# Rows stored once in float32 and split where a block gathers them, and early blocks' three products summed in one PSUM region

## The chip, the cores and the metric

The kernel runs on one core of one Trainium2 chip. That core has a matrix engine (TensorE, called PE in the profile), three engines for elementwise work (VectorE is DVE, ScalarE is ACT, GpSimd is POOL) and SyncE (SP), whose queue issues most of the transfers. The metric is the device time of one execution in microseconds; lower is better. Matrix products accumulate in PSUM, everything else lies in SBUF or, through DMA, in DRAM.

## The reference

Three layers follow one another. Attention with 8 batches, 8 heads, 576 tokens and head size 64 goes through 32 packed queries per head: `p_packed = sm_attn(p, k, v)` and `out = sm_attn(q, p_packed, p_packed)`. A dense layer takes the 4608 tokens of width 512: `h = max(x @ w1, x @ w2, x @ w3)`, then `y = h @ w_out`. The last layer picks one of 8 experts per token:

```python
logits = x @ w_gate
e_idx = np.argmax(logits, axis=1)
...
gate_w = probs[np.arange(N), e_idx]
eom = 1.0 / (1.0 + np.exp(-(x @ w_output_gate)))
for e in range(E):
    mask = e_idx == e
    ...
    h = np.maximum(x[mask] @ w1[e], 0.0)
    ye = h @ w2[e]
    out[mask] = gate_w[mask, None] * eom[mask, e, None] * ye
```

Inputs and output are float32. The kernel keeps that accuracy with float16 products by splitting a number into a high half (its float16 rounding) and a low half (what is left), and by adding three products: high with high, high with low, low with high. `PASS` in the code is that list.

## The kernel before

The first stage goes through the eight batches. For each batch the program forms scores, the packed result (`att_pv`: 4 groups of heads, each a chain of 15 matrix products over 5 chunks of keys, of which the fifth, `vt16`, has 64 keys where the others have 128), the second softmax, and the dense layer: `att_g` makes products G of the packed values with the three weights, `mm1` multiplies them by the attention weights and takes the maximum, and `mm2` multiplies a tile of 128 tokens by `w_out`, with the two gates' weights folded in as 16 more columns. There are 36 such tiles; each takes 36 products of 264 columns and a two-bank PSUM buffer `pss`, of which there are two, shared with the third product of `mm1` and with the scores.

What `mm2` does with a finished tile is the row store. Before the change, a tile was made ready for float16 work at once: the largest magnitude is found (`peak`, on ACT or DVE), a factor is worked out (`bound`, two small DVE steps), ACT writes the scaled high half (`row(0)`), ACT writes the 16 logits, DVE writes the scaled low half (`less` into `row(1)`) and only then gives the PSUM buffer back, POOL writes the factor and copies 8 logits to `LG`. The row of 512 high halves, 512 low halves, 16 logits and a factor goes to the DRAM table `yrow`. For the last five tiles (`busy`) the halves are made through an SBUF copy `ys` and POOL makes the low half.

The second stage is the expert layer in blocks of 128 tokens of one expert. From `LG` the program works out each token's expert and place (`chosen`, `ranked`, `rows_hot`, `inverse`: a matrix product of one-hot rows, line 377 of the profile, gives each block's list of tokens). This happens first for the first 27 tiles, which fills blocks 0 to 3, and then for all 36, which gives the lists of blocks 4 to 36. A block gathers its rows from `yrow` by an indirect DMA (`fetch`, POOL), transposes them by DMA (`turn_rows`), multiplies by the expert's first weights (`hidden`, two halves `fq`), takes the positive part and splits it, and multiplies by the second weights (`outer`). Its result is scaled by `gates` and sent to the output (`send`). Block i's `outer` stands on PE behind block i+1's `hidden`. The expert weights are split beforehand into the DRAM table `wscr` in 8 parts for each expert (`part_load`, `part_hi`, `part_lo`, `part_store`); for the rarer experts this is done beside the early blocks (`beside`).

In `hidden` before the change a 128-row weight block multiplies both halves of the rows at once (256 columns), then the low weights multiply the high halves (128 columns). High-with-low lands in a PSUM region of its own, so the two regions are added afterwards: `second` copies one to SBUF on ACT, `both` adds the other on DVE, then `relu_hi` (ACT) and `relu_lo` (DVE) run from SBUF.

The order of the first stage and of blocks 0 to 3 on every engine is set when the program is built: the class `Flow` takes steps with costs and ranks and lays them out one after another. The table `T_` holds its numbers. Where it sees PE pausing it inserts products of ones whose result nobody uses (`fill`, line 253). Each engine then runs its list in order. From block 4 on the order is written out by hand.

## Time and profile before

| what | value |
|---|---|
| median of 3 runs | 1019.18 us (1016.92 to 1020.22) |
| the profiled execution | 1020.05 us, of which 1018.3 us from the first to the last instruction |
| PE busy | 927.3 us, 91% of the span |
| DVE, ACT, POOL busy | 652.5, 468.6, 407.6 us |
| mean granted PE clock | 0.964 of 2.4 GHz |

A matrix product's busy time in the profile is modelled and overlaps its neighbours', so the distance between starts tells more than the duration of one. An engine that works is not always the one that sets the end: what counts is which engine is waited for in a given stretch. The profile's chain of what ended last only follows the final 50 us of transfers, so the rows below come from other views.

### The profile page before, as it was taken

The page shows a single profiled execution, that of the slowest core. Times are in us where ns is not written, and L with a number is a line of the kernel's source. Part 1 is how long each engine was busy: PE and PEld are TensorE (multiplying, and loading weights), DVE is VectorE, ACT ScalarE, POOL GpSimd, SP SyncE. Part 2 cuts the span into 40 slices and gives each one's busy share as a digit, 9 for nine tenths or more (in the row PEclk, how much of TensorE's full clock was granted, in tenths as well). Part 3 has the DMA queues.
Part 4 walks back from the last instruction along what each step waited for, and adds up shares of the span by engine and source line. Part 5 has one row for each costly group of instructions (what it writes and reads, how often), then busy time and mean ns, then how long its engine had stood idle before and what let it go on. Part 6 is the DMA issues. An engine that isn't in the chain of part 4 may idle for free. (4 is left out here: it accounts for less than half of the span.)

```text
span 1018.3 us, 23704 instructions
## 1 busy us (share of the span) xinstructions
PE 927.3 (91%) x8697; PEld 673.8 (66%) x8697; DVE 652.5 (64%) x1590; ACT 468.6 (46%) x1018; POOL 407.6 (40%) x542
## 2 busy tenths in 40 slices
PE   8879987899898797988999997999999999999995
PEld 6556764677676575766768785667676766767672
DVE  3999886745757378889695539577785344443431
ACT  4545745545555445454434353455563333333331
POOL 0534854724766368666743262223222211212110
PEclk9989998999999897989899998999999999999998
DMA  9896397570767759978912376832223593324930
GB/s 282 275 266 176 79 199 162 130 197 11 174 129 162 160 162 254 266 252 236 254 43 69 141 200 252 264 98 75 75 74 96 166 309 74 85 73 118 286 109 25
DMA packets 220985, 164.41 MB, mean 161 GB/s; under 512 B 156031, under 2 KB 195967, under 8 KB 217792
## 3 DMA queue, kind: packets, MB, share of 16 engines
q1 hardware_dynamic: 214944, 143.38, 53.2%
q0 software_dynamic: 5920, 19.46, 5.7%
q8 instruction: 70, 1.15, 0.5%
q14 instruction: 51, 0.42, 0.1%
HBM read 240.35 MB, written 53.00 MB: 288 GB/s over the span
## 5 line engine op out<-in xcount | busy, mean ns | idle before, releaser
L1024 PEld LDWEIGHTS <-G 128*128 128x128 f16 x1728 | 170.8, 100 | 84.2 <-issue 34.9
L1365 PE MATMUL pso<-wbuf,h 128*128 128x512 f16 x816 | 181.7, 379 | 0.0
L1024 PE MATMUL psm<-A,G 128*128 128x288 f16 x1152 | 167.1, 295 | 11.0 <-ACT t L197 5.1
L1062 PE MATMUL pss<-wo,hT 128*128 128x264 f16 x1296 | 152.8, 280 | 7.8 <-DVE row L217 4.3
L1314 PE MATMUL psh<-xT,wbuf 128*128 128x256 f16 x1056 | 158.5, 273 | 0.5 <-DMA wbuf<-wscr 0.5
L1365 PEld LDWEIGHTS <-h 128*128 128x128 f16 x888 | 85.3, 98 | 96.5 <-issue 0.3
L1062 PEld LDWEIGHTS <-hT 128*128 128x128 f16 x1296 | 128.4, 99 | 31.1 <-issue 10.4
L1375 POOL DMA_INDIRECT out<-o,sidx x33 | 39.5, 1198 | 259.0 <-ACT o L1370 254.6
L215 POOL TENSOR_TENSOR hT<-t,hT 128x288 f16<-128x288 f32 x89 | 72.0, 810 | 121.3 <-ACT hT L197 98.7
L1314 PEld LDWEIGHTS <-wbuf 128*128 128x128 f16 x1184 | 105.0, 98 | 17.3 <-DMA wbuf<-wscr 2.4
L1328 DVE TENSOR_TENSOR hs<-psh,hs 128x512 f32<-128x512 f32 x66 | 45.5, 690 | 90.3 <-ACT hs L197 86.5
L1024 PE MATMUL pss<-A,G 128*128 128x288 f16 x576 | 88.7, 292 | 15.0 <-ACT e L805 6.1
L1316 PE MATMUL psh<-xT,wbuf 128*128 128x128 f16 x1056 | 102.0, 219 | 0.0
L1316 PEld LDWEIGHTS <-wbuf 128*128 128x128 f16 x1184 | 91.5, 98 | 6.8
L1336 DVE SCALAR_TENSOR_TENSOR h<-hs,h 128x512 f16<-128x512 f32 x74 | 51.2, 692 | 48.8 <-ACT h L1333 48.7
L1333 ACT ACTIVATE h<-hs 128x512 f16<-128x512 f32 x74 | 46.5, 629 | 59.8 <-DVE hs L1328 59.0
L1033 DVE SCALAR_TENSOR_TENSOR t<-psm,t 128x288 f32<-128x288 f32 x96 | 43.4, 453 | 45.2 <-PE psm L1024 31.2
L197 ACT ACTIVATE hs<-psh 128x512 f32<-128x512 f32 x66 | 39.2, 594 | 63.9 <-PE psh L1316 63.9
L197 ACT ACTIVATE hT<-t 128x288 f16<-128x288 f32 x81 | 35.7, 440 | 69.2 <-DVE t L1033 69.1
L197 ACT ACTIVATE G<-psm 128x384 f16<-128x384 f32 x96 | 43.6, 485 | 32.8 <-PE psm L996 25.3
L217 DVE SCALAR_TENSOR_TENSOR G<-psm,G 128x384 f16<-128x384 f32 x96 | 49.8, 545 | 8.4 <-ACT G L197 7.8
L197 ACT ACTIVATE t<-psm 128x288 f32<-128x288 f32 x96 | 38.6, 402 | 33.3 <-PE psm L1024 24.6
(294 smaller groups left out, 1466.2 us busy)
## 6 DMA issues: line engine op xcount, KB each, us to landing
wbuf<-wscr SPq DMA_DIRECT2D x148, 1024.0 KB
pt<-in_moe_w SPq DMA_DIRECT2D x40, 512.0 KB
wscr<-po SPq DMA_DIRECT2D x40, 512.0 KB
pl<-in_moe_w SPq DMA_DIRECT2D x48, 256.0 KB
wscr<-po SPq DMA_DIRECT2D x48, 256.0 KB
ld<-in_k SPq DMA_DIRECT2D x14, 512.0 KB
ld<-in_q SPq DMA_DIRECT2D x14, 512.0 KB
ld<-in_v SPq DMA_DIRECT2D x12, 512.0 KB
```

The lines of the kernel that those rows point to most:

```text
L197: act.activation(out=o, in_=i, func=AF.Copy, scale=scale)
L215: engines[e].tensor_tensor(out=o, in0=i, in1=hi, op=ALU.subtract)
L217: dve.scalar_tensor_tensor(out=o, in0=i, scalar=scale, in1=hi, op0=ALU.mult, op1=ALU.subtract)
L1024: pe.matmul(ps()[:, 0:288], lhsT=a.G[ft]()[:, g, lg, w * 128:(w + 1) * 128], rhs=a.A16()[:, g, la, c * 288:(c + 1) * 288], start=(n == 0), ...
L1033: e0 = add(costs(288, dve=1), lambda e, src=src, o=o: dve.scalar_tensor_tensor(out=o()[:], in0=src(), scalar=sc, in1=t0()[:], op0=ALU.mult ...
L1062: pe.matmul(view()[:, nh, 0:OG0], lhsT=hT()[:, ft, lh, c0:c0 + 128], rhs=wo16()[:, ft, lw, nh, :], start=(i == 0 and ft == 0), stop=(i == ...
L1314: pe.matmul(o.rearrange("r (l t) -> r l t", l=2), lhsT=w1v[:, kt, 0, cols], rhs=xT[:, :, kt, :], start=(kt == 0), stop=False)
L1316: pe.matmul(o[:, 0:128], lhsT=w1v[:, kt, 1, cols], rhs=xT[:, 0, kt, :], start=False, stop=(kt == 3))
L1328: dve.tensor_tensor(out=hv, in0=parts_of(ps)[:, :, 0, :], in1=hv, op=ALU.add)
L1333: act.activation(out=h2_part(h2, fq, 0), in_=ps[:], func=AF.Relu)
L1336: dve.scalar_tensor_tensor(out=h2_part(h2, fq, 1), in0=ps[:], scalar=0.0, in1=h2_part(h2, fq, 0), op0=ALU.max, op1=ALU.subtract)
L1365: pe.matmul(po, lhsT=h2[:, lh, ft, :], rhs=w2v[:, ft, lw, :], start=(n == 0), stop=(n == 23))
```

## The change

Six edits go together.

- `mm2` stores a row in float32 in one step (`put`, ACT or DVE): two halves of 264, each 256 values and 8 logits, scaled by `FC`. POOL or ACT copies 8 logits to `LG`. Nothing is split there, and the five last tiles go the same way.
- A block scales and splits its rows after the gather: `bound` (a DVE reduction and two small steps), `row_hi` (ACT), `row_lo` (DVE), then the transposing DMA. `gates` takes the factor from `bound`.
- Blocks 0 to 13 sum the three products in one PSUM region (`hidden`: 12 products of 128 columns for each 128 outputs), and `relu_hi` and `relu_lo` read PSUM. Blocks from 14 on keep the old form, now `hidden_apart` and `summed`.
- The fifth chunk of `att_pv` has its lower 64 rows filled with zeros (a POOL memset for each of 6 batches), and all 15 products use 128 rows.
- Four of the eight parts of the fourth expert's weights move from the planned stage to block 4, and the fifth expert's parts from blocks 4 to 6 to blocks 5 and 6.
- A few numbers of `T_` change, so the planner lays the first stage out anew.

```diff
-T_ = dict(fg=0.597, ff=0.42, fm=2.856, rk=2.0, ...
+T_ = dict(fg=0.597, ff=0.42, fm=2.856, rk=0.088, ...
...
-            out = []
+            out = [add(dict(pool=0.4), lambda e: pool.memset(a.v16()[1][64:128], 0.0), after=[opened], rank=rank)]
...
-                        kk = 128 if t < 4 else 64
-                        vs = a.v16()[0][:, lv, t, 2 * hp:2 * hp + 2, :] if t < 4 else a.v16()[1][:kk, lv, 2 * hp:2 * hp + 2, :]
+                        vs = a.v16()[0][:, lv, t, 2 * hp:2 * hp + 2, :] if t < 4 else a.v16()[1][:, lv, 2 * hp:2 * hp + 2, :]
                         pe.matmul(ps()[:, hp * 64:hp * 64 + 64], lhsT=vs,
-                                  rhs=a.PT()[:kk, hp // 2, lp, t, (hp % 2) * 64:(hp % 2) * 64 + 64],
+                                  rhs=a.PT()[:, hp // 2, lp, t, (hp % 2) * 64:(hp % 2) * 64 + 64],
...
-            def bound(e):
-                dve.tensor_scalar(out=am()[:], in0=am()[:], scalar1=1e-30, scalar2=2.0 ** -8 if by[0] == "act" else 0.25,
-                                  op0=ALU.max, op1=ALU.mult)
-                dve.reciprocal(out=rs()[:], in_=am()[:])
...
+            def put(e):
+                o = rf().rearrange("r (n c) -> r n c", n=2)
                 if e == "act":
...
+                    act.activation(out=o, in_=view()[:, :, 0:OG0], func=AF.Copy, scale=FC[:, t:t + 1])
                 else:
...
+                    dve.tensor_scalar(out=o, in0=view()[:, :, 0:OG0], scalar1=FC[:, t:t + 1], scalar2=None, op0=ALU.mult)
+            y = add(costs(ROW, act=1, dve=1), put, after=[prev], rank=rank + V('y', batch), take=(rf,), give=(ps,))
+            f = add(dict(pool=0.25, act=0.2), lambda e: scaled(e, LG[:, t, :], rf()[:, 256:OG0]), after=[y], rank=rank + V('y', batch))
...
+    def bound(i):
+
+        am[i], rs = sm_.tile([128, 1], F32, tag="am", name="bam", bufs=6), sm_.tile([128, 1], F32, tag="rs", name="brs")
+        dve.tensor_reduce(out=am[i][:], in_=y_of(G_[i]), op=ALU.max, axis=AX.XY, apply_absolute_value=True)
+        dve.tensor_scalar(out=am[i][:], in0=am[i][:], scalar1=1e-30, scalar2=0.25, op0=ALU.max, op1=ALU.mult)
+        dve.reciprocal(out=rs[:], in_=am[i][:])
+        return rs
+
+    def row_hi(i, x, rs):
+        act.activation(out=half(x, 0), in_=y_of(G_[i]), func=AF.Copy, scale=rs[:])
+
+    def row_lo(i, x, rs):
+        less("dve", half(x, 1), y_of(G_[i]), half(x, 0), rs[:])
...
     def hidden(i, xT, fq, ps):
+
+        w1v = wbuf[i % 2][:, 0:8192].rearrange("r (a l f) -> r a l f", a=4, l=2)
+        for f4 in range(4):
+            cols = slice((fq * 4 + f4) * 128, (fq * 4 + f4 + 1) * 128)
+            for n, (lw, lx) in enumerate(PASS):
+                for kt in range(4):
+                    pe.matmul(ps[:, f4 * 128:(f4 + 1) * 128], lhsT=w1v[:, kt, lw, cols], rhs=xT[:, lx, kt, :],
+                              start=(n + kt == 0), stop=(n == 2 and kt == 3))
...
+        y = add(dict(dve=0.95), lambda e: rs.append(bound(i)), after=[y], rank=1)
+        y = add(dict(act=0.65), lambda e: row_hi(i, x(), rs[0]), after=[y], rank=1, take=(x,))
+        y = add(dict(dve=0.7), lambda e: row_lo(i, x(), rs[0]), after=[y], rank=1)
+        turned[i] = add(dict(sp=0.6), tr, after=[y], rank=1, move=0.9, give=(x,))
...
-    for u in range(8):
-        part_steps(NP1, u, found + [opened])
+
+    for i in range(NE):
+        hidden_steps(i)
+        if i == 1:
+            for u in range(4):
+                part_steps(NP1, u, hid[i] + [opened])
...
+                if i in beside:
+                    hidden(i, X_[i], fq, ps)
+                else:
+                    hidden_apart(i, X_[i], fq, ps)
+                    ps = summed(ps)
...
         for i in range(NE, NBLK0):
+            if i + 1 in split:
+                X_[i + 1] = turn_rows(split[i + 1])
+            parts_out()
             cur = block(i)
-            parts_out()
+            if i + 3 < NBLK0:
+                G_[i + 3] = fetch(i + 3)
+            if NE + 2 < i + 2 < NBLK0:
+                split[i + 2] = split_rows(i + 2)
             parts_made(i)
-            if i + 3 < NBLK0:
-                gather(i + 3)
```

PE's list where the blocks begin, first before the change: line 1365 is block 0's `outer`, line 253 the fill, line 377 the product that gives the lists of blocks 4 and up, line 1314 block 2's `hidden`.

```order
L1365 MATMUL psm<-wbuf_8766,h_9214 128x512
L253 LDWEIGHTS ones_62
L253 MATMUL psv<-ones_62 128x128
...
L377 LDWEIGHTS er_8771
L377 MATMUL psv<-fu_8781,er_8771 128x78
...
L1314 LDWEIGHTS wbuf_8766
L1314 MATMUL pss<-xT,wbuf_8766 128x256
```

And now, at the same place: line 1309 is block 2's `hidden`.

```order
L1309 LDWEIGHTS wbuf_8543
L1309 MATMUL pss<-xT,wbuf_8543 128x128
L377 LDWEIGHTS er_8548
L377 MATMUL psv<-fu_8558,er_8548 128x78
...
L1309 LDWEIGHTS wbuf_8543
L1309 MATMUL pss<-xT,wbuf_8543 128x128
```

The 40 fill products between block 0's `outer` and line 377 are gone, the first half of block 2's `hidden` (48 products) stands there instead, and the second half follows line 377.

POOL's list at the same place, before: line 373 forms one of the two operands (`fu`) of line 377, line 1375 is `send`, line 1298 `fetch`.

```order
L1095 COPY LG<-row 128x8
L215 TENSOR_TENSOR row<-ys,row 128x512
L332 MEMSET goes_8772 128x80
L333 MEMSET goes_8772 128x8
L1375 DMA out<-o,gidx_66 4608x512
L373 TENSOR_TENSOR fu_8781<-fq_8780,tokb 128x36x39
L1298 DMA g<-yrow,gidx 128x529 x2
```

And now (`send` is line 1377, `fetch` line 1267):

```order
L204 TENSOR_SCALAR LG<-row 128x8 x3
L332 MEMSET goes_8549 128x80
L333 MEMSET goes_8549 128x8
L373 TENSOR_TENSOR fu_8558<-fq_8557,bat_104 128x36x39
L1377 DMA out<-o,gidx_66 4608x512
L1267 DMA g<-yrow,gidx 128x528 x2
```

The operand is now made ahead of block 0's `send`, no low half of a row is made on POOL, and it is the other operand that POOL makes; DVE makes this one.

DVE's list where the second count begins, before: line 316 ends the choice of experts for the last nine tiles, lines 342 and 343 are the running count, lines 1328 and 1336 are `both` and `relu_lo`.

```order
L316 CAST oh_8770<-over 128x72
L1328 TENSOR_TENSOR hs<-pss,hs 128x512
L1336 SCALAR_TENSOR_TENSOR h_9214<-hs,h_9214 128x512
L1328 TENSOR_TENSOR hs<-pss,hs 128x512
L342 COPY inc_8773<-cnt 128x8
L343 SCALAR_TENSOR_TENSOR run_8774<-goes_8772,inc_8773 128x80
```

And now: line 1337 is `relu_lo`, lines 1346 to 1359 are block 0's `gates`.

```order
L316 CAST oh_8547<-over 128x72
L1337 SCALAR_TENSOR_TENSOR h_8982<-pss,h_8982 128x512 x2
L342 COPY inc_8550<-cnt 128x8
L1346 TENSOR_REDUCE bmx<-g 128x1
...
L1359 SCALAR_TENSOR_TENSOR bfac<-bfac,bam 128x1
L343 SCALAR_TENSOR_TENSOR run_8551<-goes_8549,inc_8550 128x80
```

Both `relu_lo` of block 0 and its whole `gates` now stand ahead of the running count, while no `both` is left there.

## Rows read from the trace of the kernel before

**Rows 1.** The page's first part: busy time of PE.

```profile
PE 927.3 (91%) x8697; PEld 673.8 (66%) x8697; DVE 652.5 (64%) x1590; ACT 468.6 (46%) x1018; POOL 407.6 (40%) x542
```

**Rows 2.** Windows: length, busy PE, PEld, DVE, ACT, POOL, clock, DMA.

```profile
0.00:604.34 604.34, 533.67 (x5363) 399.71 (x5364) 427.95 (x915) 299.44 (x676) 321.28 (x466) 0.95 0.68 177
604.34:654.35 50.01, 42.79 (x408) 32.09 (x406) 37.25 (x100) 20.32 (x39) 13.19 (x11) 0.93 0.78 275
654.35:1008.00 353.65, 350.86 (x2929) 242.01 (x2927) 187.31 (x575) 148.88 (x304) 73.08 (x66) 1.00 0.44 124
```

**Rows 3.** Window: an early stretch of the first stage, same columns.

```profile
24.00:96.00 72.00, 60.34 (x620) 41.28 (x621) 70.20 (x139) 37.49 (x87) 31.65 (x37) 0.93 0.87 248
```

**Rows 4.** Timeline of PE in a run of `att_pv`: start, length, products.

```profile
429.83 0.29 PE L864 MATMUL psv<-PT,v 128*128 128x64 f16 x4
430.05 0.20 PE L864 MATMUL psv<-PT,vt 64*128 64x64 f16 x1
430.18 0.29 PE L864 MATMUL psv<-PT,v 128*128 128x64 f16 x4
```

**Rows 5.** Line 864: its products on 64 rows; durations in ns.

```profile
L864 PE MATMUL psv<-PT,vt x72: 199/200/233, 136.9 to 490.7; 64*128 64x64 f16 x72
```

**Rows 6.** Timeline of DVE and POOL where the blocks begin.

```profile
622.43 1.60 DVE L371 TENSOR_TENSOR fq<-blk,iorow 128x1404 f16<-128x1404 f16 x1
...
622.95 4.35 POOL L1375 DMA_INDIRECT out<-o,gidx  x1 [14.32 <-ACT o L1370]
...
626.92 3.00 DVE L1347 SCALAR_TENSOR_TENSOR bog<-beq,bm,g 128x8 f32<-128x8 f32 x1
...
627.33 2.55 POOL L373 TENSOR_TENSOR fu<-fq,tokb 128x1404 f16<-128x1404 f16 x1
```

**Rows 7.** Waits of PE on the row store: total us, times, longest.

```profile
PE pss L1062 <- DVE row L217: 4.3, 6, 1.8
PE pss L1024 <- DVE row L217: 3.6, 3, 2.1
...
PE pss L1062 <- DVE yam L1084: 1.9, 1, 1.9
```

**Rows 8.** Groups by line: count, busy us, mean ns, idle before.

```profile
L1328 DVE TENSOR_TENSOR hs<-psh,hs 128x512 f32<-128x512 f32 x66 | 45.5, 690 | 90.3 <-ACT hs L197 86.5 <-issue 3.8
...
L217 DVE SCALAR_TENSOR_TENSOR row<-pss,yrs,row 128x512 f16<-128x512 f32 x31 | 22.9, 740 | 9.7 <-ACT row L1089 9.5
...
L1105 ACT ACTIVATE row<-pss,yrs 128x512 f16<-128x512 f32 x31 | 21.3, 686 | 12.2 <-DVE yrs L1086 11.5 <-POOL po L204 0.5
...
L1079 ACT ACTIVATE row<-pss 128x512 f32<-128x512 f32 x29 | 17.2, 592 | 34.8 <-DMA yrow<-row 16.3 <-PE pss L1062 12.5 <-issue 4.1
```

**Rows 9.** Timeline of PE where the blocks begin.

```profile
611.47 0.39 PE L1314 MATMUL pss<-xT,wbuf 128*128 128x256 f16 x2 [1.40 <-DMA wbuf<-wscr]
...
621.72 2.40 PE L253 MATMUL psv<-ones 128*128 128x128 f16 x40
629.93 2.50 PE L377 MATMUL psv<-fu,er 128*128 128x78 f16 x36 [5.82 <-DVE bog L1347]
632.23 1.05 PE L1314 MATMUL pss<-xT,wbuf 128*128 128x256 f16 x4
...
638.71 5.34 PE L1365 MATMUL psm<-wbuf,h 128*128 128x512 f16 x24
```

**Rows 10.** Timeline of PE in a steady block of the second stage.

```profile
806.07 5.34 PE L1365 MATMUL pso<-wbuf,h 128*128 128x512 f16 x24
811.25 0.60 PE L1314 MATMUL psh<-xT,wbuf 128*128 128x256 f16 x4
811.69 0.39 PE L1316 MATMUL psh<-xT,wbuf 128*128 128x128 f16 x4
811.91 0.60 PE L1314 MATMUL psh<-xT,wbuf 128*128 128x256 f16 x4
```

**Rows 11.** Window: one block with four weight parts beside it.

```profile
727.86:738.32 10.46, 10.46 (x90) 7.26 (x89) 8.55 (x18) 6.44 (x12) 2.88 (x2) 1.00 0.17 55
```

More of the change, by code (lines that the diff above doesn't have):

```diff
@@ L1049, in segments, with mm2 @@
             return out
-        def mm2(t, ready, rank, give=(), busy=False):
+        def mm2(t, ready, rank, give=()):
             hT, batch = hTs[t // 9], t * 128 // S
@@ L1181, in products, with rows @@
             hs[b] = out
-        def rows(b, busy=False):
+        def rows(b):
             tiles = [t + (b // 2) * 9 for t in (range(0, 4) if b % 2 == 0 else range(4, 9))]
@@ L1566, in block2 @@
             send(i, scale_out(i, po[:], f))
-        beside = {}
-        for r, blocks in ((4, (4, 5, 6)), (5, (7, 8, 9)), (6, (10, 11)), (7, (12, 13))):
-            load_of(r)
-            needs[r] = nc.values_load(need[0:1, r:r + 1], engines=eng, min_val=0, max_val=NT)
-            for u in range(8):
-                beside.setdefault(blocks[u * len(blocks) // 8], []).append((r, u))
-        parts, made, made_of = {}, [], []
+        parts, made, made_of, split = {}, [], [], {}
         def parts_in(i):
```

141 lines of the change are left out of this document (59 added, 82 removed).

## The prediction

> **What bounds the kernel now.** I start with the page's first part: PE is busy 91% of the span, far ahead of DVE, ACT and POOL [rows 1]. An average over stages doesn't say what a change is worth, so the next view is the windows by stage [rows 2]. The reader is to see three different kernels in them. From 654 us on PE is busy 350.86 of 353.65 us at a clock of 1.00, DVE about half of the time: this stage only gets shorter if PE's own work does. Up to 604 us PE is idle for 70.7 us, and its mean clock is 0.95, which is another 604 x 0.05 = 30 us of lost work. Between them lie 50 us in which the blocks begin, with 7.2 us idle and a clock of 0.93. So PE bounds the second stage, and in the first one PE and the engines that feed it take turns: in one stretch DVE is busy 70.20 of 72 us [rows 3]. What can be gained lies ahead of 654 us. The chain of what ended last covers only the final transfers, so it is no help here.
>
> **The fifth chunk of the attention products.** The timeline of PE shows a group of five products: four on 128 rows, then one on 64, then the next four [rows 4]. The group begins at 429.83 and the next at 430.18, a period of 0.35 us. Four on 128 rows last 0.29 us together, and one lasts 0.20 [rows 5], so three gaps make 0.09, 0.03 each: five in a row would take 0.15 us. The change of row count costs the other 0.20 us, before and after the odd one. There are 72 such products [rows 5], so with 128 rows throughout PE loses 72 x 0.20 = 14.4 us of work at full clock. I see no reason for a loss: the columns stay the same. The six memsets on POOL are not in the trace; each is bounded by nothing below and 2.55 us above (POOL's product of two operands of 1404, the nearest row [rows 6]), at most 15 us on an engine with 283 us idle in this stage. How much of 14.4 us becomes time? PE goes straight on to ready work in most cases, but each engine's later waits take some of it back. I take 8 us, a little over half, with 3 and 14.4 as the bounds.
>
> **The row store.** Three rows of the waits name it: PE waits 9.8 us for DVE's low half or factor [rows 7]. The chain that holds the PSUM buffer is a peak on ACT (592 ns), two small DVE steps, the high half on ACT (686), the low half on DVE (740) [rows 8]: 2.0 us of work and four handovers. It becomes one step over 528 columns, which I put at 0.7, just under the low half. A tile arrives every 4 us (36 x 264 columns at 2.4 GHz) with two buffers, so this wait should go. Over 31 tiles DVE also sheds 22.9 us of low halves, 5% of its 428 us [rows 2, 8], and ACT a peak of 17.2 us and high halves of 21.3 in all for some 30 single steps of 0.7; the planner spends part of it by moving casts from ACT to DVE. I take 8 us: most of the waits, and DVE's relief set against the wait that comes next. Bounds 2 (the buffer is free, but PE then waits for the maximum of `mm1`) and 12.
>
> **Where the blocks begin.** Block 0's `outer` ends at 621.72, then come 2.40 us of fill, 5.82 of idling, line 377 for 2.30, and block 2's `hidden`, which takes 6.48 us at the lowered clock instead of a steady block's 8 x 0.66 = 5.28; it ends at 638.71 [rows 9, 10]. What is waited for is POOL's operand, which ran from 627.33 for 2.55 us behind a `send` that took 4.35, though its own input was ready at 624.03 [rows 6]. Now it goes ahead of the `send`. I also expect the 1.40 us wait for block 1's weights [rows 9] to go, since their loads now leave before three of the last row stores and before the weight parts, so `outer` ends at 620.3 and half a `hidden` more at 622.95. On DVE the list up to line 371 loses three `both` (690 ns each [rows 8]) and a weight part, and gets block 0's second `relu_lo` in front: some 2 us earlier by my estimate, ready at 622. POOL's operand is then done at 624.6. DVE's own, 1.6 us like line 371, stands behind block 1's `gates`; one step of `gates` took 3.00 us while POOL formed its operand [rows 6]. That gives 626.2 to 628.5 for line 377; I take 627.5, and with 2.3 us for it and 2.9 for the second half, `hidden` ends at 632.7, 6 us earlier. The bounds are 0 (operands 3 us later than now) and 11.9 (no waiting at all: 626.8).
>
> The Trainium skill, SBUF — State Buffer, section Who interferes with whom, says that a DVE instruction with two SBUF inputs contends with a GpSimd one that reads SBUF, and that the first holds the port for its whole length. The trace agrees: that step of 3.00 us ended at 629.92 and POOL's at 629.88. By this rule line 377 comes at the late end, and this term would be 5 us instead of 6.
>
> The rows of block 4 come later after the gather than before, by a reduction, a high half and a low half, some 2.4 us by the rows of the old store [rows 8]. Their cover is the 15.6 us that two `outer` and one `hidden` take behind block 2's [rows 10]; I count four weight parts and a `gates` on DVE ahead of them, and come out 4 us early. The same three steps stand beside each later block two blocks ahead of use.
>
> **The second stage.** PE's columns are the same in both forms. The steady block shows 4 products of 256 columns in 0.44 us and 4 of 128 in 0.22 [rows 10]: 0.66 together, and 12 x 0.055 = 0.66. I put 0.5 us on 14 blocks for the seams. On DVE a block with four weight parts holds 8.55 us of 10.46 [rows 11]. It loses two `both` (1.38), gets a low half (0.74) and a reduction with two small steps (under 1.5, twice a low half): 9.4, and with a wait for the high half on ACT 10.1. That stays under PE's period, and a `relu_lo` has over 5 us until `outer` needs it, so I cost it at nothing. Blocks from 14 on have no parts and more room. The fourth expert's later parts are made at block 4, also inside this room.
>
> **The sum.** 8 + 8 + 6 - 0.5 = 21.5 us less than the profiled execution's 1020.05: 998.5. The median of the runs is 0.9 us lower, so I predict 998.
>
> **Rivals.**
> *Weights too slow (slower).* In the early blocks all 96 products of `hidden` have 128 columns, each with its own weight load, where half had 256 before. If loads cannot keep up in a long run, PE pays in 14 blocks. The forecast's gain is used up at 21.5 / (14 x 96) = 16 ns a product, 71 instead of 55. At the 110 ns that a product of 256 columns takes, it would be 74 us more, 1072. Against it stand four in 0.22 us [rows 10] and 40 fills in 2.40, 0.06 each with the tail [rows 9]; for it, only that no run of 96 is in the trace. The Trainium skill, TensorE: Matmul & The Clock Gate, section Back-to-back issue gap, gives about 81 ns for a stream of load and product at 128 columns, against 56 for one alone; by it, as an estimate, 14 x 96 x 26 ns = 35 us more, 1033. No row here shows 81. Chance 4%.
>
> *The re-laid first stage waits elsewhere.* The order of every engine ahead of 604 us is new. A single late load or a `t` buffer can cost 2 to 5 us, and each longer pause lowers the clock as well. With half of the first two terms gone, 1006; with nearly all, 1012. In favour: 70.7 us of idling are spread over many releasers, of which the row store is 9.8. Chance 19% for 1006 to 1016. If it loses more than the edits give, the time is unchanged (6%) or above 1022 (4%).
>
> *All of it counts.* 14.4 + 12 + 10 = 36 us less, 984: PE's work is the limit almost everywhere, and shorter pauses save clock too. Chance 12% for under 990.
>
> *DVE becomes the bound beside the early blocks.* At 11.5 us instead of 10.1 in the 10 blocks, after the 5 us of slack, it costs 5 to 6 us, 1004: inside the range and counted in the forecast.
>
> **How the numbers follow.** The forecast (990 to 1006) has 55%, less gain 19%, more 12%, no change 6%, slower 8%. The range, 983 to 1013, leaves out the two worst cases, 14%, and a few per cent of the tails. I take 0.3% (3 us) as what a measurement of this kernel can tell from no change: faster 86%, same 6%, slower 8%.
>
> **What would show it.** In the changed profile the five-product groups should repeat every 0.15 us. No wait of PE should name the row store. Block 2's `hidden` should end 20 to 24 us earlier than now, after a pause of 3 to 6 us ahead of line 377, and a steady block should still take 10.46 us on PE. I would be wrong if products in the summed form come more than 60 ns apart, if line 377 waits as long as before, or if PE's idle time ahead of 604 us is still near 70 us with new releasers.

## The result, and the profile after

The changed kernel takes 1030.5 us (median; 1029.7 to 1031.4), the kernel before 1018.1 us in the same session: a ratio of 1.012, 95% interval 1.0098 to 1.0141. The forecast was 998, in a range of 983 to 1013, with 8% for slower. It was wrong in sign.

The profile's first part, and the windows with marks at the same events as in [rows 2] (end of the last tile, start of block 4's `hidden`, a little ahead of the end):

```profile
PE 912.6 (89%) x9120; PEld 671.3 (65%) x9120; DVE 677.4 (66%) x1630; ACT 435.3 (42%) x910; POOL 390.6 (38%) x493
```

```profile
0.00:602.37 602.37, 515.09 (x5379) 390.79 (x5380) 417.41 (x852) 264.77 (x568) 305.91 (x419) 0.96 0.67 177
602.37:646.83 44.46, 40.36 (x497) 31.50 (x495) 33.22 (x108) 12.81 (x29) 11.09 (x10) 0.96 0.74 249
646.83:1018.00 371.17, 357.19 (x3249) 248.97 (x3247) 226.77 (x671) 157.69 (x313) 73.14 (x65) 0.98 0.44 114
```

The first row's length fell by 2.0 us where I had put 16, although PE's busy time fell by 18.6: its idle time rose from 70.7 to 87.3. The second row is 5.6 us shorter. The third was the stage that nothing was to happen in. PE, which had been idle for 2.8 us there, is idle for 14, and its clock is no longer 1.00.

What PE waited for in the second stage (total us, times, longest), and three of its blocks as windows, from one `outer` to the next:

```profile
PE psh L1319 <- DMA xT<-xs: 9.8, 3, 5.1
PE psh L1309 <- DMA xT<-xs: 1.7, 2, 0.9
```

```profile
802.19:812.65 10.46, 10.46 (x91) 7.25 (x89) 5.89 (x20) 4.05 (x9) 1.72 (x3) 1.00 0.98 321
812.65:830.20 17.55, 13.15 (x92) 8.89 (x90) 6.58 (x21) 4.22 (x10) 2.83 (x3) 0.81 1.08 293
830.20:840.66 10.46, 10.46 (x92) 7.25 (x90) 6.11 (x21) 4.19 (x9) 2.05 (x2) 1.00 0.19 15
```

The wait is for the transposing transfer of a block's rows, a releaser that had no row in the kernel before. One block takes 17.55 us. In it PE stands for 4.4 us and then works for 5 us at a granted clock of 0.50, which is 1.2 of 2.4 GHz (0.81 over the block):

```profile
822.40:827.40 5.00, 5.00 (x32) 4.02 (x33) 0.00 (x0) 0.00 (x0) 1.04 (x1) 0.50 0.98 402
```

The DMA share is 0.98 in the block ahead of it and 1.08 in this one, and 0.19 in the next. A second such block of 18.06 comes at 956 us, and four early ones are 0.4 to 1.2 us too long.

I add up, from the starts of the first product of each `outer`, how much the blocks from the second on exceed 10.46 us: 0.8 us before the change, 18.5 after. With 2.0 us less to the last tile, 0.7 less from there to block 0's `outer`, 5.0 less from it to block 1's, and 0.6 more behind the last block, this gives +10.6, the whole difference of the two profiled executions (1030.71 and 1020.05).

What was issued around the long block, and PE's first product after it:

```profile
803.41 4.48 SPq L1262 DMA_DIRECT2D wbuf<-wscr  x4
811.04 1.76 SPq L1293 DMA_TRANSPOSE xT<-xs  x1
814.16 4.20 SPq L1262 DMA_DIRECT2D wbuf<-wscr  x4
```

```profile
822.40 1.01 PE L1319 MATMUL psh<-xT,wbuf 128*128 128x256 f16 x4 [4.40 <-DMA xT<-xs]
```

From 803.4 to 807.6 four weight loads of 1 MB are issued, since a new expert's blocks begin. DVE's low half of the rows ends at 811.01, and at 811.04 their transfer is issued; its block would begin at 817.9, but its data arrive at 822.3. Counted from the trace's packets in some of the microseconds: the loads' (8192 bytes) and the transposition's (256 bytes).

```
us     8192 B   256 B
808        51       0
810        51       0
812        53       0
814        47       0
816        19     125
817         3      79
818         0     507
819         3     200
```

The transposition moves one packet in the five microseconds after its issue, and the others when the loads are nearly through. Before the change such a transfer was issued two blocks earlier, right behind the gather. The one of the kernel before whose block began at 821.71 had 24 us:

```profile
797.31 1.26 SPq L1304 DMA_TRANSPOSE xT<-g  x1
```

The boundary came out close to what I had worked out. The lines that answer to [rows 9] and [rows 6]:

```profile
613.91 5.34 PE L1367 MATMUL psm<-wbuf,h 128*128 128x512 f16 x24
619.09 2.84 PE L1309 MATMUL pss<-xT,wbuf 128*128 128x128 f16 x48
625.44 1.93 PE L377 MATMUL psv<-fu,er 128*128 128x78 f16 x36 [3.51 <-DVE nbf L1512]
627.17 4.04 PE L1309 MATMUL pss<-xT,wbuf 128*128 128x128 f16 x48
```

```profile
619.33 2.54 POOL L373 TENSOR_TENSOR fu<-fq,bat 128x1404 f16<-128x1404 f16 x1 [15.39 <-DVE fq L371]
...
619.45 2.44 DVE L1347 SCALAR_TENSOR_TENSOR beq<-g,bmx,rev 128x8 f32<-128x8 f32 x1
...
623.77 1.61 DVE L373 TENSOR_TENSOR fu<-fq,tokb 128x1404 f16<-128x1404 f16 x1
```

The wait ahead of line 377 fell from 5.82 to 3.51 us, and half a `hidden` stands in front of it. The row names line 1512 as the releaser, but it began at 625.30 and has nothing to do with line 377; DVE's operand `fu` ended at 625.38.

The five-product groups of the attention products repeat every 0.15 us, as forecast:

```profile
344.13 0.19 PE L864 MATMUL psv<-PT,vt 128*128 128x64 f16 x1
344.16 0.28 PE L864 MATMUL psv<-PT,v 128*128 128x64 f16 x4
344.28 0.19 PE L864 MATMUL psv<-PT,vt 128*128 128x64 f16 x1
```

And what PE waited for in the first stage, the largest entries:

```profile
PE psm L1024 <- DVE G L217: 13.0, 11, 3.8
PE psm L1024 <- ACT t L197: 11.9, 7, 2.9
PE psm L996 <- DVE G L217: 9.2, 8, 4.9
PE pss L1024 <- ACT e L806: 9.0, 5, 7.8
PE pss L1062 <- ACT row L1073: 8.1, 4, 5.5
```

Against [rows 7], the row store is still there, now with its step on ACT (30 of 36 tiles), and the four waits for G, `t` and `e` above make 43 us; the same four were 19.6 before.

### The profile page after: what moved, and what is told of

Same layout as the page of the kernel before. It is cut to its first block, busy times and chain, and to the rows that moved or that the text cites. A ratio compares the mean times of both kernels' runs of the same rounds, so it can differ in the third digit from the quotient of the medians.

```text
span 1028.9 us, 24362 instructions
## 1 busy us (share of the span) xinstructions
PE 912.6 (89%) x9120; PEld 671.3 (65%) x9120; DVE 677.4 (66%) x1630; ACT 435.3 (42%) x910; POOL 390.6 (38%) x493
## 5 line engine op out<-in xcount | busy, mean ns | idle before, releaser
L1024 PE MATMUL psm<-A,G 128*128 128x288 f16 x1152 | 164.5, 292 | 27.5 <-DVE G L217 13.0
L1319 PE MATMUL psh<-xT,wbuf 128*128 128x256 f16 x736 | 114.1, 279 | 9.8 <-DMA xT<-xs 9.8
L215 POOL TENSOR_TENSOR hT<-t,hT 128x288 f16<-128x288 f32 x84 | 66.6, 794 | 118.7 <-ACT hT L197 80.8
L1309 PEld LDWEIGHTS <-wbuf 128*128 128x128 f16 x1344 | 77.1, 99 | 6.3 <-DMA xT<-xs 3.3
L1319 PEld LDWEIGHTS <-wbuf 128*128 128x128 f16 x736 | 66.6, 100 | 21.0 <-issue 10.5
L1321 PE MATMUL psh<-xT,wbuf 128*128 128x128 f16 x736 | 72.9, 223 | 0.0
L1328 DVE TENSOR_TENSOR hs<-psh,hs 128x512 f32<-128x512 f32 x46 | 31.8, 691 | 48.6 <-ACT hs L197 48.6
L1321 PEld LDWEIGHTS <-wbuf 128*128 128x128 f16 x736 | 58.1, 100 | 5.0
L1284 ACT ACTIVATE xs<-g,brs 128x512 f16<-128x512 f32 x37 | 26.7, 722 | 77.8 <-DVE brs L1280 77.8
L197 ACT ACTIVATE hT<-t 128x288 f16<-128x288 f32 x72 | 31.7, 440 | 61.6 <-DVE t L1033 61.5
L1309 PE MATMUL psh<-xT,wbuf 128*128 128x128 f16 x960 | 55.3, 219 | 1.8 <-DMA xT<-xs 1.7
```

The costliest lines, as they stand in the source:

```text
L197: act.activation(out=o, in_=i, func=AF.Copy, scale=scale)
L215: engines[e].tensor_tensor(out=o, in0=i, in1=hi, op=ALU.subtract)
L1024: pe.matmul(ps()[:, 0:288], lhsT=a.G[ft]()[:, g, lg, w * 128:(w + 1) * 128], rhs=a.A16()[:, g, la, c * 288:(c + 1) * 288], start=(n == 0), ...
L1309: pe.matmul(ps[:, f4 * 128:(f4 + 1) * 128], lhsT=w1v[:, kt, lw, cols], rhs=xT[:, lx, kt, :], start=(n + kt == 0), stop=(n == 2 and kt == 3))
L1319: pe.matmul(o.rearrange("r (l t) -> r l t", l=2), lhsT=w1v[:, kt, 0, cols], rhs=xT[:, :, kt, :], start=(kt == 0), stop=False)
L1321: pe.matmul(o[:, 0:128], lhsT=w1v[:, kt, 1, cols], rhs=xT[:, 0, kt, :], start=False, stop=(kt == 3))
```

## The experiments

Theory A: the second stage loses because the transposing transfer is issued so late that weight loads stand in front of it. Rival B: the summed products or DVE's new steps are too slow beside the early blocks. For the first stage, theory C: the reliefs are real, but this stage is a relay of five engines and transfers, so little of a relief becomes time. Rival D: the planner's new order is simply a bad one.

Ratios are to the kernel before in the same session, with 95% intervals; its median was 1018.1 to 1021.3 us there, and its row below has the first session's. One per cent is 10.2 us. The column on blocks is the excess over 10.46 us worked out above; the last column is the start of the last tile's first product.

| kernel | median us | ratio | excess of blocks, us | last tile at, us |
|---|---|---|---|---|
| before | 1018.1 | 1 | 0.8 | 600.3 |
| after | 1030.5 | 1.012 (1.0098 to 1.0141) | 18.5 | 598.3 |
| e1_early_turn | 1010.8 | 0.9916 (0.9885 to 0.9947) | 0.9 | 596.3 |
| e2_late_turn | 1025.9 | 1.007 (1.0049 to 1.0091) | 7.6 | 598.7 |
| e11_other_queue | 1035.1 | 1.0163 (1.0112 to 1.0215) | 25.1 | 592.1 |
| e12_apart_form | 1032.1 | 1.0118 (1.0096 to 1.014) | 21.1 | 598.2 |
| e8_all_summed | 1012.0, one run | | 2.9 | 595.9 |
| e3_64_rows | 1025.8 | 1.0072 (1.0046 to 1.0097) | 9.0 | 603.4 |
| e5_early_64 | 1017.7 | 0.9989 (0.9964 to 1.0014) | 1.0 | 603.4 |
| e4_pad_alone | 1018.0 | 0.9975 (0.9952 to 0.9998) | | 599.7 |
| e6_long_store | 1033.7 | 1.0153 (1.0113 to 1.0194) | | 612.9 |
| e9_light_store | 1019.4 | 0.9991 (0.9971 to 1.0011) | | 599.8 |
| e10_light_and_pad | 1018.2 | 0.9981 (0.9956 to 1.0007) | | 598.1 |
| e7_old_numbers | 1013.2 | 0.9932 (0.9902 to 0.9963) | | 598.3 |
| e13_fewer_products | 1014.5 | 0.995 (0.9924 to 0.9976) | | 589.6 |
| e14_pool_relieved | 1009.9 | 0.9899 (0.9842 to 0.9956) | | 590.0 |
| e15_gates_later | 1010.5 | 0.9897 (0.9867 to 0.9927) | 1.6 | 597.1 |

Five of these kernels have the very first stage of the changed one (after, e1, e8, e11, e12); their last tiles start at 592.1 to 598.3, mean 596.2. One execution's start of the last tile is thus no better than some 6 us, and small differences of it are not read here. Of the blocks behind, most repeat to 0.1 us.

### The transfer one block earlier: e1_early_turn

```diff
-            if i + 1 in split:
-                X_[i + 1] = turn_rows(split[i + 1])
+            if NE + 2 < i + 2 < NBLK0:
+                X_[i + 2] = turn_rows(split_rows(i + 2))
             parts_out()
             cur = block(i)
             if i + 3 < NBLK0:
                 G_[i + 3] = fetch(i + 3)
-            if NE + 2 < i + 2 < NBLK0:
-                split[i + 2] = split_rows(i + 2)
```

> The changed kernel with one edit: rows are split and their transposing DMA is issued one block earlier (for block i+2 where it was block i+1). Theory A: the second stage loses because this transfer waits in SP's queue order behind four 1 MB weight loads when a new expert's weights come, and lands after the block needs it; PE should then lose no block period longer than 11 us from block 7 on, and the time falls by the 14 to 17 us that PE lost there, to 1014 to 1017 us. Rival B: the 12 products of 128 columns in the early blocks, or DVE's added steps, are what costs; DVE's work and PE's products stay the same here, so the time stays within 3 us of 1030.

The time went from 1.2% above the kernel before to 0.8% below it, 1010.8 us. PE has no wait in the second stage, at a clock of 1.00:

```profile
645.00:1000.00 355.00, 351.00 (x3246) 246.19 (x3242) 224.95 (x665) 159.90 (x313) 72.62 (x64) 1.00 0.47 120
```

PE's idle 4 us in this window lie behind the last block. The excess of the blocks fell by 17.6 us, the ratios differ by 2.0% or 20.8 us (17 to 25 by their intervals): more than the 14 to 17 that I had expected, and in keeping with the 17.6. DVE carries the same steps and PE the same products, so B is not what cost the 17.6.

### The late transfer alone: e2_late_turn

```diff
             G_[i] = fetch(i)
-            X_[i] = turn_rows(G_[i])
...
-            cur = block(i)
+            if NE + 2 < i + 1:
+                if i + 1 < NBLK0:
+                    X_[i + 1] = turn_rows(G_[i + 1])
             parts_out()
+            cur = block(i)
             parts_made(i)
...
                 gather(i)
+                X_[i] = turn_rows(G_[i])
```

> The kernel before with one edit: the transposing DMA of a block's rows is issued where the changed kernel issues it, at the start of the block before the one that uses it, instead of right behind the gather two blocks earlier; nothing is split later and the products keep their old form. Theory A: the same two blocks in which a new expert's weights are loaded late in the run (about 20 and 33) stretch by 4 to 7 us each and the time rises by 8 to 16 us, to 1026 to 1034. Rival B: no change (1018), since neither DVE's steps nor the form of the products are here.

The kernel before, with this moved (and the stores of the weight parts with it), is 0.7% slower, and its waits show the changed kernel's releaser, which the kernel before has nowhere:

```profile
PE psh L1314 <- DMA xT<-g: 3.8, 3, 2.8
```

The 7.1 us are just under the lower end of what I expected: here the transfer leaves as soon as SP comes to it, 10.0 us ahead of its use in the block that corresponds to the one above, where the changed kernel first has the split to wait for and has 6.9 us. Blocks 19 and 33 stretch by 0.9 and 4.6 us, three others by 0.5 to 0.7.

### Another queue: e11_other_queue

```diff
-    def turn_rows(x):
+    def turn_rows(x, q=None):
         xT = xp.tile([128, 2, 4, 128], F16, tag="xT", name="xT")
-        sp.dma_start_transpose(
+        (q or sp).dma_start_transpose(
...
-                X_[i + 1] = turn_rows(split[i + 1])
+                X_[i + 1] = turn_rows(split[i + 1], act)
```

> The changed kernel with the late transposing DMA issued from ACT in place of SP, at the same place of the program. If the transfer is late because it stands in one queue behind the weight loads, it now passes them and the long block periods near block 20 and 33 go: 1010 to 1016. If it is late because the loads fill the DMA engines whatever the queue, the periods stay and the time is 1026 to 1032.

Theory A as I had first put it, that the transfer waits its turn in SP's queue, falls. The page lists these transfers under a queue of their own, and yet the excess is 25.1 us and the time 1035.1, above even the 1026 to 1032 that I gave for this case. At 784 us the same thing happens:

```profile
q10 hardware_dynamic: 31680, 7.87, 5.0%
```

```profile
782.64 23.42 SPq L1262 DMA_DIRECT2D wbuf<-wscr  x8
...
783.94 1.39 ACTq L1293 DMA_TRANSPOSE xT<-xs  x1
...
792.91 1.01 PE L1319 MATMUL psh<-xT,wbuf 128*128 128x256 f16 x4 [5.01 <-DMA xT<-xs]
```

Of the eight loads in that row the first two, at 782.64 and 783.76, had 2.1 MB to move just then. The transposition, issued at 783.94 from ACT, has its first packets move at 788, and 758 of its 1024 in the microsecond from 791, when no load packet is left; it is 5.0 us late. So what holds it is that loads are already under way, whatever the queue. The cure is time, not a queue. The Trainium skill, DMA: Bandwidth & Descriptors, section Issuing engines are not separate DMA queues, says that spreading transfers over issuing engines saves issue time only; the trace agrees, in that the data came no sooner.

### The old form in the early blocks: e12_apart_form

```diff
-                if i in beside:
+                if False:
                     hidden(i, X_[i], fq, ps)
```

(on the kernel of e1_early_turn)

> The changed kernel with the early transposition, and blocks 4 to 13 in the old form of the first product (two PSUM regions, added on ACT and DVE), so that DVE has the new splitting and the old adding beside the weight parts, some 10 to 11 us in a block of 10.46. If DVE then becomes the bound, the early periods with four parts rise over 10.54. If not, they read 10.46 and the time is 0.5 to 1 us less than with the summed form.

```profile
PE psh L1319 <- DVE hs L1328: 16.3, 9, 3.0
```

```profile
673.00:686.57 13.57, 13.10 (x102) 8.36 (x100) 10.60 (x25) 7.75 (x14) 2.91 (x2) 1.00 0.23 60
```

2.0% slower than with the summed form: periods of 11.1 to 15.2 us in blocks 6 to 14, with PE waiting for `both`, which frees its PSUM buffer. DVE is busy 10.60 of 13.57 us there, and 9.8 of 12.8 on the average of these nine blocks, so its total alone is not the limit; I take it to be the row of steps that DVE and ACT hand to each other, which no run separates. With the summed form (e1_early_turn) the same blocks hold DVE for 7.0 to 9.2 of 10.54 us. The summed form is what makes room for the split.

### The summed form in all blocks: e8_all_summed

```diff
-                if i in beside:
+                if True:
                     hidden(i, X_[i], fq, ps)
```

(on e1_early_turn)

> The changed kernel with the early transposition, and the summed form (12 products of 128 columns) in all blocks in place of the first 14. Theory: a block in this form takes 10.54 us on PE where the other takes 10.46, so 23 more blocks cost 1.9 us and every period reads 10.54. Rival: DVE's load or the weight loads make the early period, then the late blocks, with less beside them, keep 10.46.

```profile
812.98 5.52 PE L1309 MATMUL psh<-xT,wbuf 128*128 128x128 f16 x96
818.34 3.83 PE L1367 MATMUL pso<-wbuf,h 128*128 128x512 f16 x17
```

From block 1's `outer` on all periods but one (10.67) are 10.54 us: 0.08 us more a block, whatever stands beside it. 96 products take 5.36 us from start to start, 55.8 ns each. The rival "weights too slow" is out. The Trainium skill, TensorE: Matmul & The Clock Gate, section Back-to-back issue gap, gives about 81 ns for such a stream; the trace disagrees.

### The zero rows of the attention products: e3_64_rows, e5_early_64, e4_pad_alone

The changed kernel with 64 rows again, e5 on e1_early_turn:

```diff
+                        kk = 128 if t < 4 else 64
...
-                                  rhs=a.PT()[:, hp // 2, lp, t, (hp % 2) * 64:(hp % 2) * 64 + 64],
+                                  rhs=a.PT()[:kk, hp // 2, lp, t, (hp % 2) * 64:(hp % 2) * 64 + 64],
```

> The changed kernel with the fifth chunk of the attention products back at 64 rows; every engine's order is that of the changed kernel, the memsets stay. By the prediction's term the time rises by 8 us (3 to 14.4), to 1038. Rival: in the new order PE waits for DVE and ACT anyway, the 14 us of PE work lie in those waits, and the time stays within 2 us of 1030.

It got 0.5% faster, with its last tile 5 us later and 9.5 us less excess in the same blocks: how long a transfer is late varies with where the loads happen to stand. In the block that took 17.55 us above and takes 11.70 here, the first load is issued 0.9 us and the transposition 1.0 us earlier, counted from the `outer` ahead of it. So the next one has the transfers early:

> The changed kernel with the early transposition (the first experiment's edit), and the fifth chunk of the attention products back at 64 rows; order kept. In the experiment with 64 rows and late transpositions PE's last tile began 5 us later but the late blocks waited less, so the two were mixed. Theory A (padding is worth some 5 us in this order, the shorter total came only from shorter transfer waits): 1014 to 1018 us, and all block periods at 10.46 to 10.54. Rival (the products on 128 rows cost something elsewhere): 1008 or less.

0.73% above e1_early_turn, 7.4 us (3 to 11 by the two intervals), close to the prediction's 8. Then the kernel before with the zero rows, the memset within an existing step, so that nothing is laid out anew:

```diff
-                    out.append(add(costs(512, dve=1, both=1), lambda e, t=t: less(e, a.v16()[1][0:64, 1], t()[0:64], a.v16()[1][0:64, 0], 32.0),
+                    def low(e, t=t):
+                        pool.memset(a.v16()[1][64:128], 0.0)
+                        less(e, a.v16()[1][0:64, 1], t()[0:64], a.v16()[1][0:64, 0], 32.0)
+                    out.append(add(costs(512, dve=1, both=1), low,
```

> The kernel before with the zero rows and the products on 128 rows alone; every engine's order stays, POOL gets six memsets. By the prediction's term the time falls by 8 us (3 to 14.4), to 1010. Rival: in an order laid out with the longer products the relief goes into the waits behind them, and the time stays within 2 us of 1018.

2.5 us (0.2 to 4.9), nearer the rival than the term of 8; the six memsets take 0.95 us each. The same 14 us of PE work are worth 7.4 us where they are put back into an order that was laid out without them, and 2.5 where they are taken out of an order that was laid out with them; the intervals of the two overlap, so that the difference between them is not well shown.

### The row store: e6_long_store, e9_light_store

e6 lengthens it in the changed kernel with early transfers:

```diff
+                am = mp.tile([128, 1], F32, tag="yam", name="yam", bufs=3)
+                act.activation(out=o[:, :, 0:256], in_=yv(), func=AF.Abs, accum_out=am[:])
+                dve.scalar_tensor_tensor(out=o[:, :, 0:256], in0=yv(), scalar=am[:], in1=o[:, :, 0:256], op0=ALU.mult, op1=ALU.subtract)
                 if e == "act":
```

> The changed kernel with the early transposition, and the row store made long again in the same order: ahead of the one step that stores a row stand a pass on ACT (absolute values with their sum) and a pass on DVE that reads PSUM, so that a tile holds its PSUM buffer for three passes as before the change, and DVE and ACT carry the old load (35 x 0.7 us each); the stored row is the same. By the prediction's term for the row store the time rises by 8 us (2 to 12), to 1019. Rival: PE waits for other results of DVE and ACT at these places anyway, and the rise is under 2 us.

24 us slower than e1 by the ratios (19 to 29), the last tile 16.7 us later: some three times the term. e9 lightens it in the kernel before:

```diff
             def peak(e):
                 by.append(e)
+                if not busy:
+                    return
...
             def bound(e):
+                if not busy:
+                    return
...
-                h = add(costs(512, act=1), lambda e: act.activation(out=row(0), in_=yv(), func=AF.Copy, scale=rs()[:]), after=[pk], rank=rank + V('y', batch))
+                h = add(costs(512, act=1), lambda e: act.activation(out=row(0), in_=yv(), func=AF.Copy, scale=FC[:, t:t + 1]), after=[pk], rank=rank + V('y', batch))
...
-                l = add(costs(512, dve=1), lambda e: less(e, row(1), yv(), row(0), rs()[:]), after=[h, lg], rank=rank + V('y', batch), give=(ps,))
+                l = add(costs(512, dve=1), lambda e: dve.memset(row(1), 0.0), after=[h, lg], rank=rank + V('y', batch), give=(ps,))
```

> The kernel before with a light row store in its own order: for 31 of the 36 tiles (all but the last five) the peak, its two small steps and the low half are left out (the factor of the token stands in for the scale, the low halves are zero), so a tile holds its PSUM buffer for one pass and the logits on ACT, and DVE loses some 23 us of low halves and 8 of small steps, ACT some 18. By the prediction's term the time falls by 8 us (2 to 12), to 1011. If relief given to an order laid out without it is lost in the next wait, as the zero rows were in the kernel before, it falls by under 3 us.

0.9 us (from 3.0 gained to 1.1 lost). The waits of [rows 7] are gone from the kernel; 2.8 us of waiting for the logits on ACT have come in their place, and little or nothing came of it in time. DVE's relief is smaller than I had expected: the zeros take 8.4 us, and its busy time up to the last tile falls by 17 us (428 to 411), ACT's by 18.

### Both reliefs, and what holds them: e10, e13, e14

e10 has the edits of e4 and e9 in the kernel before.

> The experiment before with the zero rows of the attention products as well: both reliefs of the first stage in the order of the kernel before. By the prediction's terms 16 us less than before, 1003. If the order holds the relief back, 1013 to 1018.

1.9 us (from 4.5 gained to 0.7 lost), where the prediction's two terms say 16. In its trace the freed waits stand elsewhere; against the entries of [rows 7]:

```profile
PE psm L999 <- DVE G L217: 11.8, 6, 6.6
PE psm L1027 <- ACT t L197: 8.2, 3, 4.1
PE pss L1027 <- ACT e L808: 7.8, 1, 7.8
PE psv L253 <- ACT pp L892: 7.5, 3, 4.6
```

In the kernel before these four were 6.4, 5.1, 6.1 and 2.8 us. Followed back, in one execution of each kernel, from the last tile's last product by the rule of the profile's chain (at each step to what released it, or to the instruction before it on its engine), us by engine:

```
before             PE 231.7  DVE 142.7  DMA 76.0  issue 52.0  SPq 40.8  POOL 30.9  ACT 28.2
e10_light_and_pad  PE 195.6  DVE 121.9  DMA 90.0  issue 41.1  SPq 46.0  POOL 86.4  ACT 19.2
e14_pool_relieved  PE 233.7  DVE 129.7  DMA 83.6  issue 42.4  SPq 49.2  POOL 36.7  ACT 17.0
```

PE is busy 534 of 604 us in this stage and carries 232 of some 600 us of the chain. With PE and DVE relieved, POOL's share grows from 31 to 86. Two experiments ask whether that reading is right. e13 takes 10 of the 36 products of each tile away:

```diff
-                        for ft in range(NFT):
+                        for ft in range(NFT) if i < 2 else (NFT - 1,):
```

> The kernel before, leaving out 10 of the 36 products of each of the 36 tiles in mm2 (most of the low-with-high pass), in the same order: 360 products of some 0.11 us, 40 us less work on PE ahead of the last tile. If PE's work sets the length of the first stage, the time falls by 30 us or more, to 990 or less. If PE mostly waits its turn in a relay with DVE, ACT, POOL and the transfers, as the small effect of the zero rows says, it falls by under 15 us in the first 500 us of the run, and what is gained comes from the last 100 us, where PE was busy 98%.

5.1 us (2.4 to 7.7) for 40 us of PE's work. Up to 500 us PE is busy 410.73 us where it had 431.20 (first line, the kernel before), and idle for the difference:

```profile
0.00:500.00 500.00, 431.20 (x4382) 319.53 (x4383) 364.46 (x749) 254.73 (x567) 271.87 (x394) 0.94 0.75 191
...
0.00:500.00 500.00, 410.73 (x4134) 297.76 (x4135) 367.42 (x756) 256.11 (x572) 274.36 (x395) 0.92 0.75 190
500.00:593.67 93.67, 90.01 (x872) 69.29 (x870) 62.11 (x159) 43.17 (x105) 45.35 (x72) 1.00 0.36 116
```

The last tile starts 10.7 us earlier, block 0's `outer` only 4.0 and block 1's 6.8: ahead of the first PE waits 5.7 us for the weights of block 1, where it had waited 1.4 [rows 9]. So the first stage gave back about 11 of the 40 us, and the boundary kept only a part of that.

e14 is e10 with POOL relieved of the low halves of the values:

```diff
+                        def low4(e, t=t, hs=hs, x=x):
+                            if e == "pool":
+                                return pool.memset(a.v16()[0][:, 1, x, hs, :], 0.0)
+                            less(e, a.v16()[0][:, 1, x, hs, :], t()[:, :, x, :], a.v16()[0][:, 0, x, hs, :], 32.0)
+                        out.append(add(costs(256, dve=1, both=1), low4,
```

> The kernel before with the light row store and the zero rows (the tenth experiment), and in addition POOL's low halves of the values replaced by zeros (38 steps, some 45 us of POOL less): the low halves of these chunks are left out of the result. Followed back from the last tile, the chain of waits in the tenth experiment has 86 us of POOL where the kernel before has 31. If POOL took over as what is waited for, the time falls by 4 to 12 us, to 1006 to 1014. If DVE and the transfers hold it just as well, it stays within 3 us of 1018.

0.82% better than e10, 8.4 us (2 to 15 by the two intervals), with 41 us less on POOL. The stage up to the last tile, e10 and then e14 (length, busy PE, PEld, DVE, ACT, POOL, clock, DMA):

```profile
0.00:602.10 602.10, 517.80 (x5363) 390.13 (x5364) 409.67 (x851) 280.63 (x618) 328.01 (x472) 0.95 0.68 177
0.00:594.00 594.00, 513.94 (x5363) 389.53 (x5364) 404.66 (x851) 280.74 (x618) 287.09 (x434) 0.97 0.69 180
```

An engine that is busy 54% of that stage gave, by the medians of the ratios, four times as much as the two reliefs of the change together. DVE's busy time fell by 5 us as well, over the same 851 steps, so that a part of the gain may come from DVE's steps having grown shorter beside a lighter POOL and not from POOL being waited for; no run separates the two. For the order of the kernel before C holds: little of a relief of PE, DVE and ACT becomes time there, and a relief of another engine does.

### The planner's numbers: e7_old_numbers

```diff
-T_ = dict(fg=0.597, ff=0.42, fm=2.856, rk=0.088, ...
+T_ = dict(fg=0.597, ff=0.42, fm=2.856, rk=2.0, ...
```

(the whole table of before, on e1_early_turn)

> The changed kernel with the early transposition, and the planner's table with the numbers of before, so that the first stage is laid out in another order with the same work. If the new order itself is what loses the relief of PE, this gains several us: 1000 to 1006. If it is only one of many orders in which DVE and ACT are waited for, it lies within 6 us of 1011 on either side, and PE's idle time ahead of the last tile stays over 70 us.

1.6 us slower by the ratios, with overlapping intervals, and PE is idle for 84 us up to its last tile, where e1_early_turn has 81. So it is not these few numbers that lose the relief. Rival D is not out by this. Putting back the 64 rows costs the new order 7.4 us (e5) and a long row store 24 (e6), so it does use what it was given; yet its last tile comes only some 3 us earlier than in the old order. Either the new order is worse apart from the two reliefs, or work put into an order laid out without it costs more than it is worth. That some quite different order would keep more is open: none was tried.

### Block 1's gates behind the operand: e15_gates_later

```diff
-        gated[i] = add(dict(dve=1.5), gate, after=done, rank=200)
+        gated[i] = add(dict(dve=1.5), gate, after=done + (found1 if i == 1 else []), rank=200)
```

> The changed kernel with the early transposition, and block 1's gates on DVE placed behind DVE's operand of line 377 instead of ahead of it. PE waited 3.5 us there, and DVE's operand stood behind 4.4 us of gates, of which one step took 2.44 us while POOL formed the other operand. If this order is the wait, line 377 follows the first half of block 2's hidden after under 1 us, and the time falls by 2.5 to 3.5 us, to 1007 to 1008. Rival: POOL's operand, or the two operands slowing one another, takes the place of the gates, and under 1.5 us are gained.

```profile
622.13 1.49 PE L377 MATMUL psv<-fu,er 128*128 128x78 f16 x36 [1.34 <-POOL fu L373]
```

```profile
618.11 3.97 POOL L373 TENSOR_TENSOR fu<-fq,tokb 128x1404 f16<-128x1404 f16 x1 [15.39 <-DVE fq L371]
```

Line 377's wait fell from 3.5 to 1.3 us and block 1's `outer` follows block 0's after 13.4 us instead of 17.1, of which later blocks gave back 0.7. In the times it can't be told from e1_early_turn (0.9897 and 0.9916, overlapping). Theory and rival were both right: the gates were the wait, and the operands then slowed one another. POOL's took 3.97 us beside DVE's, 2.54 beside the step of the gates.

## Why the prediction was wrong, point by point

**The second stage: the step that failed.** I put +0.5 us. The seams of the summed form cost 0.08 us a block, some 1 us in all where I had 0.5. But I wrote that the late split's "three same steps stand beside each later block two blocks ahead of use" and counted DVE's and ACT's time in them, and not the transfer that follows. In the program they stand two blocks ahead, but on DVE they come behind the `gates` of that block, so that the low half ends, and the transfer is issued, two thirds of a block ahead of use (6.9 us). Before the change it was issued 2.3 blocks ahead (24 us). I worked that cover out for block 4 alone. The row of the kernel before that would have warned me is a block in which a new expert's weights come, with a DMA share of 1.04; I had read one with weight parts, at 0.17 [rows 11]:

```profile
816.53:826.99 10.46, 10.46 (x91) 7.27 (x89) 4.85 (x17) 3.58 (x8) 2.03 (x2) 1.00 1.04 391
```

Nothing waited there then, since the rows had been transposed long before. The late transfer cost 17.6 us (e1), and the same move alone costs the kernel before 7.1 (e2).

**The attention products: mechanism right, price right in the new order and too high in the old.** The group takes 0.15 us, as worked out. As time it is 2.5 us in the old order and 7.4 in the new one (I had 8, bounds 3 and 14.4).

**The row store: the term that failed next.** One step of 0.7 us, as I put it; it takes 693 ns on ACT. (The waits for the old store were 12.1 us, not 9.8: three shorter entries of 1.7, 0.4 and 0.2 us belong to it as well.) But "this wait should go" did not make 8 us: in the old order PE's waits for it gave way to others as long (e9, e10), and in the new order PE still waits 8.4 us for the one step. In the new order the change's two first terms together gave 3 us: last tiles at 596.2 on average, against 599.5 in the two executions with the old order. That is within the spread of single executions, but the times say the same: of the 8.6 us that e1_early_turn gained, 5.0 are the boundary. The rival "the re-laid first stage waits elsewhere" had this, with 1006 to 1016 and 19%; e1_early_turn, which leaves only it, is at 1010.8. The sign that I had named for being wrong came out too: PE's idle time in this stage is 87.3 us, with new releasers.

**The boundary: right in sum, and in part by luck.** My 6 us were counted from the last tile to the end of block 2's `hidden`; there 0.7 + 5.0 = 5.7 came out. Line 377 starts 23.2 us behind the end of the last tile, as in the forecast, and not at the late end that I gave with 5 us. But a wait of 0.6 us for block 1's weights stayed where I had all 1.4 go, and the second half of `hidden` took 3.87 us where I had put 2.9, while line 377 took 1.73 and not 2.3. The Trainium skill, SBUF — State Buffer, section Who interferes with whom, says that of two such instructions the one that comes first holds the shared port for its whole length. Two traces agree, one in each direction: POOL's 2.54 us became 3.97 in e15 behind an operand of 1.63 us that DVE had started 0.05 us ahead of it, and DVE's step of 128x8, 0.23 us elsewhere, took 2.44 behind POOL in the changed kernel. In the kernel before it does not follow from the starts: DVE's step of 3.00 us begins 0.41 us ahead of POOL's operand and still ends with it [rows 6].

**DVE beside the early blocks: right.** It holds 7.0 to 9.2 us of 10.54 (e1_early_turn), where I had put 9.4; with the old form it would not have fitted (e12).

## What to carry to other kernels

When a step is put later, follow it to the end of its transfer, and give that transfer the time that it needs behind the largest loads that can be under way, not the time of its issue: here a quarter of a megabyte issued behind 4 MB arrived 11 us later, and another queue did not help. In a stage where several engines take turns, a relief is worth what the chain of waits gives that engine; take work away in an experiment before counting on it (here 40 us less on PE gave 5 us, 41 less on POOL gave 8). A busy share of 91% over a run says little on a stage in which PE is idle for 70 us.

## What the runs showed of the hardware

A transposition issued from another engine's queue did not get past 2.1 MB of loads that were issued 1.3 and 0.2 us ahead of it: none of its 1024 packets moved in the first four microseconds, and 758 moved in the one after the loads had ended (e11). The next one, issued at 794.92 with no loads about, moved all its packets between 796 and 798. A pause of PE of 4.4 us was followed by 5 us at a granted clock of 0.50 (1.2 of 2.4 GHz), in which eight products took 1.28 us where they take 0.66 at 1.00, so that the pause cost 7.1 us in all.
